# The first blocks of the last down products as half-array pairs, put between and behind the last gate groups

## The chip, the cores and the metric

The kernel runs on one core of one Trainium2 chip. The metric is the device time of one execution in microseconds; the time of a kernel is the median of several runs. Before the change it is 202.91 us, from three runs of 202.81 to 202.94. A profile is one execution recorded instruction by instruction; its span runs from the first to the last recorded instruction.

## The reference

The reference is a transformer block on an input `x` of 2048 tokens by 448 columns in bf16: a layer norm and a linear attention with 16 heads, added to `x` to give `h`, and then the part that the change touches, a gated feed-forward layer on the normed `h` with 1792 inner columns:

```
def _B_ref(x, w_gate, w_up, w_down):
    g = jnp.einsum("bsd,df->bsf", x, w_gate)
    u = jnp.einsum("bsd,df->bsf", x, w_up)
    h = _sigmoid(g) * u
    return jnp.einsum("bsf,fd->bsd", h, w_down)
...
h2 = h + _B_ref(_layernorm(h, axis=-1), B_w_gate, B_w_up, B_w_down)
```

## The kernel before

**Tiles.** The 2048 tokens are 16 tiles of 128 (tile 0 to 15), the 1792 inner columns 14 blocks of 128 (called `ff`, 0 to 13). The feed-forward part of the last four tiles, 12 to 15, is what the change touches.

**A gate group** (`gate_up`, lines 895 to 917) computes g and u of one `ff` for several tiles at once, four (512 tokens) at the end of the kernel. The contraction over 448 columns is done on half of TensorE's rows at a time: a matmul on rows 0 to 63 and one on rows 64 to 127 run beside each other, each into a bank of PSUM of its own. Line 333, in the helper `both`, issues these pairs. Operation `ga12_8` is the first part of the group of tiles 12 to 15 and `ff` 8 (four pairs), `gb12_8` the second (three pairs), with the banks exchanged between the halves. Even `ff` use banks 4 and 5, odd ones banks 0 and 1. ScalarE then takes the sigmoid of g (`sig12_8`, line 909), and VectorE multiplies it with u (`hh12_8`, line 915) and writes the product, transposed as it already is, into `hhT`. After that the two banks are free for the group of `ff` + 2.

**A down product** multiplies `hhT` with `w_down` and sums over all 14 `ff` in one bank for each tile. For tiles 0 to 11 it is done by `down` (lines 919 to 934) for two tiles at once in half-array pairs: operations `dn10_4`, `dp10_4` and so on, where the lower rows work for one tile and the upper rows for the other, and in a second pass the other way round. For tiles 12 to 15 `down1` (lines 936 to 946) does one tile at a time with matmuls on all 128 rows, issued by line 942. The 14 `ff` are split by the list `late` into blocks of 4, 4, 2, 2, 1 and 1, with names by tile and first `ff`: `dm13_8` is tile 13, `ff` 8 and 9. The banks are 2, 3, 6 and 7 for tiles 12 to 15. Tile 15 is split by columns: 320 of them as `dm15_*` in bank 7, the last 128 as `dl15_0` and `dl15_12` in bank 4. VectorE then adds the bank to `h` (`fin12`, line 949), and SyncE's queue writes the tile out (`out12`, line 952).

**Order.** The order of the operations on each engine is written out by hand in the table `ORDER` (lines 243 to 302), by name. `PROGRAM` (lines 311 to 319) creates the operations. `Graph` finds from what each operation reads and writes which others it depends on, and gives it waits on semaphores where the two are on different engines. TensorE waits for itself only where two operations write the same bank from different halves of the array (`crosses`, lines 85 to 87, from the argument `half`); an operation on the full array has an empty `half` and takes no such wait.

The order on TensorE around the change, before it:

```
dp10_8 ga12_9 dp10_11 ga12_8 gb12_9 gb12_8 dm13_0 dm12_0 ga12_11 ga12_10 gb12_11 gb12_10 dm14_0 dm15_0
dm14_4 dm13_4 ga12_13 ga12_12 gb12_13 gb12_12 dm13_8 dm12_4 dm13_10 dm15_4 dm15_8 dm12_8 dm13_12 dm12_10
dm12_12 dm12_13 dm13_13 dm14_8 dm14_10 dm14_12 dm14_13 dm15_10 dm15_12 dm15_13 dl15_0 dl15_12
```

Of the kernel before, what the change touches and what calls it, by code (L numbers as in the profile page):

```python
# [18 lines left out]
class Graph:  # L19
# [10 lines left out]
    def op(self, eng, name, fn, r=(), w=(), dma=None, nring=0, after=(), rows=128, half=None, kb=0, grp=None, many=None):  # L30
        o = _Op()
        o.engs = eng if isinstance(eng, tuple) else (eng,)
        fns = fn if isinstance(fn, tuple) else (fn,) * len(o.engs)
        k = o.engs.index(self.where[name]) if name in self.where else 0
        o.i, o.eng, o.name, o.fn, o.dma = len(self.ops), o.engs[k], name, fns[k], dma
        o.rows, o.half, o.kb, o.grp = rows, half or {}, kb, grp
        o.deps = {}
        r, w = self.flat(r), self.flat(w)
        o.need_inc, o.sem, o.val = False, None, 0

        def dep(j, raw):
            if j != o.i:
                o.deps[j] = o.deps.get(j, False) or raw
        for k in r:
            if k in self.lastw:
                dep(self.lastw[k], True)
            for j in self.adds.get(k, ()):
                dep(j, True)
        for k in w:
            if k in self.lastw:  # L50
                dep(self.lastw[k], True)
            for j in self.readers.get(k, ()):
                dep(j, False)
            if grp is None:
                for j in self.adds.pop(k, ()):
                    dep(j, True)
        for j in after:
            dep(j, False)
        if dma is not None and nring:
            lst = self.ring.setdefault(dma, [])  # L60
            if len(lst) >= nring:
                dep(lst[-nring], True)
            o.sem = (dma, len(lst) % nring)
            o.val = 16 * (len(lst) // nring + 1)
            lst.append(o.i)
        if many is not None:
            o.sem, o.val = (dma,) + many[:1], 16 * many[1]
        for k in w:
            if grp is not None:
                self.adds.setdefault(k, []).append(o.i)  # L70
                continue
            self.lastw[k] = o.i
            self.readers[k] = []
        for k in r:
            if k not in w:
                self.readers.setdefault(k, []).append(o.i)
        self.ops.append(o)
        return o.i
# [50 lines left out]
    def emit(self, nc):  # L129
# [87 lines left out]
D = 448  # L217
# [12 lines left out]
LO, HI = slice(0, 64), slice(64, P)  # L230
# [32 lines left out]
    ),  # L263
# [22 lines left out]
    ),  # L286
    "dve": (
# [14 lines left out]
    ),  # L302
    "pool": (
# [15 lines left out]
)  # L319


# [6 lines left out]
def both(e, lo, hi):  # L328
    for a in range(max(len(lo), len(hi))):
        for l, row in ((lo, 0), (hi, 64)):  # L330
            if a < len(l):
                o, w, r, st, sp = l[a]
                p = e.matmul(o, lhsT=w, rhs=r, start=st, stop=sp, tile_position=(row, 0))  # L333
    return p
# [15 lines left out]
def build(nc, A_x, A_wqkv, A_w_phi, A_wo, B_w_gate, B_w_up, B_w_down, out):  # L350
# [8 lines left out]
    NX, NO, NH, NPHI, NS, NE, NV, NSG, NHH = 5, 4, 3, 4, 4, 5, 5, 4, 2  # L359

    with ExitStack() as es:
        def sb(name, shape, d=dt.bfloat16):
            return es.enter_context(nc.sbuf_tensor(name, shape, d))
# [34 lines left out]
        wd_sb = sb("wd_sb", [P, FT, D])  # L398
# [3 lines left out]
        hhT = [sb("hhT%d" % c, [P, FT, 512]) for c in range(NHH)]  # L402
# [16 lines left out]
        def bk(i):  # L419
            return psum[:, i * 512:(i + 1) * 512]  # L420
# [4 lines left out]
        def TS(t):  # L425
            return slice((t % 4) * P, (t % 4 + 1) * P)
        g = Graph()
        op = g.op

        def B(i):  # L430
            return ("bank", i)

        def load(name, dst, src, w, kb, r=(), eng="sp", many=None):
# [9 lines left out]
           r=["ident"], w=["ident"])  # L443
# [20 lines left out]
        def opads(e):  # L464
# [4 lines left out]
           w=[("phi", s) for s in range(NPHI)])  # L469
        op("pool", "wqpad", lambda e: e.memset(W2[1][:].rearrange("p k g n -> p (k g) n")[:, :, 56:64], 0.0),  # L470
           w=[("W2", 1, kt) for kt in range(KT)])
        op("dve", "mask2", lambda e: e.tensor_reduce(mask2[:], ident[:].rearrange("p (c h) -> p h c", h=2), AX.X, ALU.add),
           r=["ident"], w=["mask2"])
# [445 lines left out]
        def down(t, b, parts):  # L919
            c = (t // 4) % NHH  # L920
            hb = hhT[c]
            for ph, a, n in parts:
                i, j = ph, 1 - ph

                def f(e, ph=ph, i=i, j=j, a=a, n=n):
                    def part(i, s):
                        return [(bk(b[i])[:, 0:D], hb[s, ff, TS(t + i)], wd_sb[s, ff, :], ph == 0 and ff == 0,
                                 ph == 1 and ff == FT - 1) for ff in range(a, a + n)]
                    return both(e, part(i, LO), part(j, HI))
                op("pe", "d%s%d_%d" % ("np"[ph], t, a), f,  # L930
                   r=[("hh", c, ff, (t + i) % 4) for ff in range(a, a + n) for i in range(2)] + [("wd", ff // 2) for ff in range(a, a + n)],
                   w=[B(b[0]), B(b[1])], rows=64, half={b[i]: 0, b[j]: 1})
            for i in range(2):
                finish(t + i, b[i])

        def down1(t, b, parts, w=0):
            hb = hhT[(t // 4) % NHH]
            for nm, b, lo, hi in (("dm", b, 0, D - w), ("dl", 4, D - w, D))[:1 + (w > 0)]:
                for a, n in parts if nm == "dm" else ((0, 12), (12, 2)):
                    def f(e, a=a, n=n, b=b, lo=lo, hi=hi):  # L940
                        for ff in range(a, a + n):
                            p = e.matmul(bk(b)[:, lo:hi], lhsT=hb[:, ff, TS(t)], rhs=wd_sb[:, ff, lo:hi], start=ff == 0, stop=ff == FT - 1)  # L942
                        return p
                    op("pe", "%s%d_%d" % (nm, t, a), f,
                       r=[("hh", (t // 4) % NHH, ff, t % 4) for ff in range(a, a + n)] + [("wd", ff // 2) for ff in range(a, a + n)], w=[B(b)])
                finish(t, b, lo, hi, "" if nm == "dm" else "b")
# [6 lines left out]

        mid = [(ph, a, n) for ph in range(2) for a, n in ((0, 4), (4, 4), (8, 3), (11, 3))]
        late = ((0, 4), (4, 4), (8, 2), (10, 2), (12, 1), (13, 1))

        for step in PROGRAM.split():
            k, _, v = step.partition(":")
            v = [int(i) for i in v.split(",") if i]
            if k == "num":  # L960
                num(*v)
            elif k == "wo":
                wout(v[0])
            elif k == "ot":
                otrans(v[0])
            elif k == "wo1":
                wout1(v[0])
            elif k == "qs":
                qsum(v[0])
            elif k == "pq":  # L970
                pq(*v)
            elif k == "kvz":
                kvmask()
            elif k == "gu":
                for ff in range(*(v[2:4] or (0, FT))):
                    gate_up(v[0], v[1], ff)
            elif k == "down":
                down(v[0], (v[1], v[1] + 1), mid)
            elif k == "down1":
                down1(v[0], v[1], late, *v[2:])  # L980

        at = {o.name: o.i for o in g.ops}
        for a, b in PACE.items():
# [5 lines left out]
def bass_sequential_preLN__linear_kernel_hedgehog__glu_gated_glu__prompt_kernel(  # L989
    nc, A_x, A_wqkv, A_w_phi, A_wo, B_x, B_w_gate, B_w_up, B_w_down, out  # L990
):
    build(nc, A_x, A_wqkv, A_w_phi, A_wo, B_w_gate, B_w_up, B_w_down, out)
# [28 lines left out]
```

## Time and profile before

| | us |
|---|---|
| median of three runs | 202.91 |
| the profiled execution | 203.01 |
| its span | 200.8 |
| TensorE busy in it | 195.0 |
| VectorE busy | 127.0 |
| ScalarE busy | 100.0 |
| GpSimd busy | 69.7 |

The profiled execution's own time is longer than its span by what lies around the instructions, about 2.2 us. PE is TensorE's matmuls and PEld its weight loads, which run beside them; DVE is VectorE, ACT ScalarE, POOL GpSimd, SP SyncE, and SPq the queue of transfers that SyncE issues. Matmuls are pipelined: one starts before the one ahead of it has ended, so the time that a matmul costs is read from the distance of starts and not from its duration. L333 is line 333 of the kernel. A timeline row gives the start, the time from the first start to the last end of the instructions merged in it, the engine, the line, the operation with its tiles, the count, and in brackets the engine's idle time ahead of it with what ended it.

### The profile page before, as it was taken

The numbers are of one execution on the slowest core, as the hardware profiler recorded it, in microseconds if no ns is written. First come the engines' busy times: TensorE is split into PE (matmuls) and PEld (weight loads), VectorE is DVE, ScalarE is ACT, GpSimd is POOL, SyncE is SP. The second block draws the span as 40 slices with busy tenths as digits, with TensorE's granted clock in tenths as the row PEclk, the third lists the DMA queues.
The fourth block names the chain that finished last, engine by engine and source line by source line (L and its number), as shares of the span: only waits on it lengthen the run. The fifth ranks groups of instructions, "written<-read, shape, count | busy, mean of one in ns | idle before, by whom it ended". The sixth has DMA issues, their size and how long they took to land.

```text
span 200.8 us, 5873 instructions
## 1 busy us (share of the span) xinstructions
PE 195.0 (97%) x2500; PEld 113.3 (56%) x2500; DVE 127.0 (63%) x309; ACT 100.0 (50%) x213; POOL 69.7 (35%) x107
## 2 busy tenths in 40 slices
PE   7899999999989999999999999999999999999994
PEld 2735555566557788886555444444555555553453
DVE  6899999978889876286558775246233522362224
ACT  3778989899795776356232543232323212221220
POOL 4599977643444456353303146100310000000000
PEclk9999999999999999999999999999999999999999
DMA  6996725469942583214102204103020000003002
GB/s 150 331 137 125 84 51 127 118 212 287 343 55 45 124 123 54 54 34 77 40 17 68 53 3 99 35 0 96 3 52 3 0 0 3 0 19 122 0 0 91
DMA packets 32866, 16.25 MB, mean 81 GB/s; under 512 B 25097, under 2 KB 31945, under 8 KB 32841
## 3 DMA queue, kind: packets, MB, share of 16 engines
q1 hardware_dynamic: 32336, 15.86, 36.5%
q8 instruction: 19, 0.31, 0.6%
q10 hardware_dynamic: 504, 0.03, 0.2%
q14 instruction: 7, 0.05, 0.1%
HBM read 8.34 MB, written 1.84 MB: 51 GB/s over the span
## 4 chain that ended last, share of the span: by engine, by line
PE 92%; DVE 3%; DMA 2%; SPq 1%; issue 1%
PE psum L333 84%; PE psum L942 5%; DMA wk_sb<-in_A_wqkv_dram 2%; PE psum L622 1%; SPq L434 1%; PE psum L531 1%; DVE c_sb L803 1%; DVE st L828 1%; PE psum L545 0%; DVE b_sb L800 0%; DVE hn_pad L850 0%; DVE xnT L538 0%; PE psum L606 0%; DVE x_sb L830 0%; DVE rsm L797 0%
## 5 line engine op out<-in xcount | busy, mean ns | idle before, releaser
L333 PE MATMUL psum<-xnT,wg_sb 64*128 64x512 bf16 (+1 forms) x490 | 95.0, 333 | 0.3 <-DVE xnT L538 0.3
L333 PE MATMUL psum<-xnT,wu_sb 64*128 64x512 bf16 (+1 forms) x490 | 94.9, 333 | 0.1
L909 ACT ACTIVATE sg_sb<-psum 128x512 bf16<-128x512 f32 (+1 forms) x70 | 35.5, 515 | 76.0 <-PE psum L333 75.6
L915 DVE TENSOR_TENSOR hhT<-sg_sb,psum 128x512 bf16<-128x512 bf16 (+1 forms) x44 | 29.2, 675 | 46.3 <-ACT sg_sb L909 45.8
L333 PEld LDWEIGHTS psum<-xnT,wg_sb 64*128 64x128 bf16 x490 | 44.5, 94 | 20.9 <-DVE hhT L915 1.1
L333 PEld LDWEIGHTS psum<-xnT,wu_sb 64*128 64x128 bf16 x490 | 44.5, 94 | 14.2 <-PE psum L333 0.9
L333 PE MATMUL psum<-wd_sb,hhT 64*128 64x448 bf16 x336 | 37.8, 349 | 0.0
L333 PEld LDWEIGHTS psum<-wd_sb,hhT 64*128 64x128 bf16 x336 | 17.9, 94 | 14.3 <-DVE x_sb L835 0.3
L333 PE MATMUL psum<-wv_sb,xnT 64*128 64x448 bf16 x112 | 22.3, 351 | 0.1
L333 PE MATMUL psum<-Wk,xnT 64*128 64x448 bf16 x112 | 22.2, 351 | 0.1
L809 POOL TENSOR_TENSOR o_pad<-c_sb,rden 128x448 bf16<-128x448 bf16 x12 | 11.2, 937 | 26.4 <-DVE rden L805 26.0
L682 POOL TENSOR_TENSOR phi<-hhT,rs 128x896 bf16<-128x896 bf16 x10 | 17.0, 1708 | 3.0 <-DVE rs L678 1.7
L672 DVE TENSOR_REDUCE ss<-hhT 128x32 f32<-128x896 bf16 x16 | 17.1, 1066 | 0.3 <-ACT hhT L669 0.2
L720 ACT ACTIVATE eq<-psum 120x1024 bf16<-120x1024 f32 x16 | 15.8, 1030 | 0.9 <-PE psum L333 0.9
L333 PE MATMUL psum<-xnT,Wq 64*120 64x512 bf16 x112 | 14.8, 384 | 0.1
L949 DVE SCALAR_TENSOR_TENSOR x_sb<-psum,x_sb 128x448 bf16<-128x448 f32 (+2 forms) x17 | 9.6, 594 | 8.1 <-PE psum L333 5.7
L914 ACT CAST xn_pad<-psum 128x256 bf16<-128x256 f32 x26 | 9.4, 375 | 6.3 <-PE psum L333 5.8
L333 PE MATMUL psum<-wo_o,oT 64*128 64x448 bf16 x49 | 11.5, 349 | 0.0
L333 PE MATMUL psum<-wo_e,oT 64*128 64x448 bf16 x49 | 11.5, 349 | 0.0
L915 POOL TENSOR_TENSOR hhT<-sg_sb,xn_pad 128x256 bf16<-128x256 bf16 x11 | 7.6, 695 | 11.1 <-ACT xn_pad L914 6.9
L942 PE MATMUL psum<-wd_sb,hhT 128*128 128x448 bf16 (+2 forms) x70 | 11.1, 316 | 0.0
L333 PEld LDWEIGHTS psum<-Wk,xnT 64*128 64x128 bf16 x112 | 7.7, 94 | 5.6 <-PE psum L333 1.0
(112 smaller groups left out, 251.3 us busy)
## 6 DMA issues: line engine op xcount, KB each, us to landing
out_dram<-x_sb SPq DMA_DIRECT2D x15, 112.0 KB, 1.8
x_sb<-in_A_x_dram SPq DMA_DIRECT2D x7, 224.0 KB, 4.9
wd_sb<-in_B_w_down_dram SPq DMA_DIRECT2D x7, 224.0 KB, 7.7
wg_sb<-in_B_w_gate_dram SPq DMA_DIRECT2D x3, 448.0 KB, 4.6
wu_sb<-in_B_w_up_dram SPq DMA_DIRECT2D x3, 448.0 KB, 4.8
wv_sb<-in_A_wqkv_dram SPq DMA_DIRECT2D x2, 224.0 KB, 5.7
wk_sb<-in_A_wqkv_dram SPq DMA_DIRECT2D x2, 196.0 KB, 3.8
wo_e<-in_A_wo_dram SPq DMA_DIRECT2D x1, 336.0 KB, 3.5
```

The lines of the kernel that those rows point to most:

```text
L333: p = e.matmul(o, lhsT=w, rhs=r, start=st, stop=sp, tile_position=(row, 0))
L434: return op(eng, name, lambda e: e.dma_start(dst, src), r=r, w=w, dma="in" if eng == "sp" else "ain", nring=(48 if eng == "sp" else 8) if ...
L531: p = e.matmul(bk(3)[:, 0:size], lhsT=zero[:, 0:P], rhs=zero[:, 0:size], start=True, stop=True)
L672: op("dve", "ss%d" % t, lambda e: e.tensor_reduce(ss[:, s, :].rearrange("p (b h) -> p b h", h=2), eks.rearrange("p b (d h) -> p b h d", h= ...
L682: return e.tensor_tensor(phi[:, sp, :, :, :].rearrange("p b a n -> p (b a) n")[:, :, 0:56].rearrange("p b (d h) -> p b d h", h=2), eks.rea ...
L720: op("act", "eq%d_%d%s" % (c, i, "pm"[sg]), lambda e, sg=sg: e.activation(eq[c][:, sg, 2 * i:2 * i + 2, :].rearrange("p g n -> p (g n)"), ...
L809: return e.tensor_tensor(o_pad[:, t % NO, off:off + D].rearrange("p (h d) -> p h d", h=H), c_sb[:, t % NS, :, 0:DH], rden[:, t % NS, :][:, ...
L909: op("act", "sig" + nm, lambda e: e.activation(sg_sb[:, k, 0:N], bk(bg)[:, 0:N], ACT.Sigmoid), r=[B(bg)], w=[("sg", k)])
L914: op("act", "uc" + nm, lambda e: e.copy(up, bk(bu)[:, 0:N]), r=[B(bu)], w=[ub])
L915: op(("pool", "dve") if nm in UCOPY else "dve", "hh" + nm, lambda e: e.tensor_tensor(hhT[(t0 // 4) % NHH][:, ff, ns], sg_sb[:, k, 0:N], up ...
L942: p = e.matmul(bk(b)[:, lo:hi], lhsT=hb[:, ff, TS(t)], rhs=wd_sb[:, ff, lo:hi], start=ff == 0, stop=ff == FT - 1)
L949: op("dve", "fin%d%s" % (t, nm), lambda e: e.scalar_tensor_tensor(out=h_sb[:, t, lo:hi], in0=bk(b)[:, lo:hi], scalar=1.0, in1=h_sb[:, t, l ...
```

## The change

Of tiles 12, 13 and 14 the first blocks of the down product (`ff` 0 to 7 of tile 12, 0 to 9 of tiles 13 and 14) are no longer full-array matmuls. A new function `downh` makes half-array pairs of two tiles: the lower 64 rows of each `ff` for one tile, the upper 64 rows for the other. The list `HALF` takes the three tiles in turn (12 with 13, 13 with 14, 14 with 12 or 13), so that each tile gets both halves of each of its `ff`. Banks stay 2, 3 and 6. The rest of these tiles and all of tile 15 stay with `down1`; the new table `left` says how many blocks it skips.

The new operations are placed on TensorE in the order below: two behind `gb12_8`, three behind `gb12_10`, two between `gb12_12` and `gb12_13`, one behind `gb12_13`. The last two gate groups change places, `dm15_0` moves behind the last gate group, and `dm13_13` moves ahead of `dm12_12`. On ScalarE and VectorE the places of `ff` 4 and 5 are exchanged, on ScalarE those of 10 and 11 too; on VectorE `fin11` moves ahead of `hh12_9`, `fin10` between `hh12_9` and `hh12_8`, and `fin13` ahead of `fin12`. SyncE's order stays.

```diff
 "act":
-        "sig12_0 sig12_2 sig12_3 sig12_4 sig12_5 sig12_7 sig12_6 sig12_9 sig12_8 sig12_10 sig12_11 sig12_12 sig12_13 "
+        "sig12_0 sig12_2 sig12_3 sig12_5 sig12_4 sig12_7 sig12_6 sig12_9 sig12_8 sig12_11 sig12_10 sig12_12 sig12_13 "
 "pe":
-        "dp10_8 ga12_9 dp10_11 ga12_8 gb12_9 gb12_8 dm13_0 dm12_0 ga12_11 ga12_10 gb12_11 gb12_10 dm14_0 dm15_0 "
-        "dm14_4 dm13_4 ga12_13 ga12_12 gb12_13 gb12_12 dm13_8 dm12_4 dm13_10 dm15_4 dm15_8 dm12_8 dm13_12 dm12_10 "
-        "dm12_12 dm12_13 dm13_13 dm14_8 dm14_10 dm14_12 dm14_13 dm15_10 dm15_12 dm15_13 dl15_0 dl15_12 "
+        "dp10_8 ga12_9 dp10_11 ga12_8 gb12_9 gb12_8 dx1213_0 dx1213_4 ga12_11 ga12_10 gb12_11 gb12_10 dx1314_0 "
+        "dx1314_4 dx1314_8 ga12_12 ga12_13 gb12_12 dx1412_0 dx1412_4 gb12_13 dx1413_8 dm15_0 dm12_8 dm13_10 dm15_4 "
+        "dm13_12 dm15_8 dm12_10 dm13_13 dm12_12 dm12_13 dm14_10 dm14_12 dm14_13 dm15_10 dm15_12 dm15_13 dl15_0 "
+        "dl15_12 "
 "dve":
-        "hh8_9 hh8_8 hh8_11 hh8_10 hh8_13 fin6 fin7 hh8_12 hh12_1 hh12_0 hh12_2 hh12_3 hh12_4 hh12_5 fin9 hh12_7 fin8 "
-        "hh12_6 fin10 fin11 hh12_9 hh12_8 hh12_10 hh12_11 hh12_12 hh12_13 fin12 fin13 fin14 fin15 fin15b "
+        "hh8_9 hh8_8 hh8_11 hh8_10 hh8_13 fin6 fin7 hh8_12 hh12_1 hh12_0 hh12_2 hh12_3 hh12_5 hh12_4 fin9 hh12_7 fin8 "
+        "hh12_6 fin11 hh12_9 fin10 hh12_8 hh12_10 hh12_11 hh12_12 hh12_13 fin13 fin12 fin14 fin15 fin15b "
 PROGRAM:
-    "down:10,6 gu:12,4 down1:12,2 down1:13,3 down1:14,6 down1:15,7,128 "
+    "down:10,6 gu:12,4 half down1:12,2 down1:13,3 down1:14,6 down1:15,7,128 "
+HALF = (
+    (12, 13, 0, 4), (12, 13, 4, 4), (13, 14, 0, 4), (13, 14, 4, 4), (13, 14, 8, 2), (14, 12, 0, 4), (14, 12, 4, 4),
+    (14, 13, 8, 2),
+)
...
+        def downh(lo, hi, a, n):
+            hb, bank = hhT[(lo // 4) % NHH], {12: 2, 13: 3, 14: 6}
+            first = {t: next(p for p in HALF if t in p[:2] and p[2] == 0) for t in (lo, hi)}
+
+            def f(e):
+                def part(t, s):
+                    return [(bk(bank[t])[:, 0:D], hb[s, ff, TS(t)], wd_sb[s, ff, :], ff == 0 and first[t] == (lo, hi, a, n), False)
+                            for ff in range(a, a + n)]
+                return both(e, part(lo, LO), part(hi, HI))
+            op("pe", "dx%d%d_%d" % (lo, hi, a), f,
+               r=[("hh", (lo // 4) % NHH, ff, t % 4) for ff in range(a, a + n) for t in (lo, hi)] + [("wd", ff // 2) for ff in range(a, a + n)],
+               w=[B(bank[lo]), B(bank[hi])], rows=64, half={bank[lo]: 0, bank[hi]: 1})
...
+        left = {12: 2, 13: 3, 14: 3, 15: 0}
...
+            elif k == "half":
+                for p in HALF:
+                    downh(*p)
             elif k == "down1":
-                down1(v[0], v[1], late, *v[2:])
+                down1(v[0], v[1], late[left[v[0]]:], *v[2:])
```

## The prediction

> **What bounds the kernel now.** The page is read first for the engine that sets the end. The lines below are its span, its busy shares, the granted clock and the chain that ended last.
>
> ```profile
> span 200.8 us, 5873 instructions
> PE 195.0 (97%) x2500; PEld 113.3 (56%) x2500; DVE 127.0 (63%) x309; ACT 100.0 (50%) x213; POOL 69.7 (35%) x107
> PEclk9999999999999999999999999999999999999999
> PE 92%; DVE 3%; DMA 2%; SPq 1%; issue 1%
> ```
>
> TensorE is busy for 195.0 of 200.8 us, holds 92% of the chain, and its clock is full in every slice. So time is won only if TensorE's own sequence gets shorter. The chain in order of time shows which part of it the change touches:
>
> ```profile
> 119.94 61.11 PE psum L333 x594
> 181.05 1.62 PE psum L942 x8
> 182.67 3.13 PE psum L333 x28
> 185.80 2.92 PE psum L942 x16
> 188.72 3.13 PE psum L333 x28
> 191.85 6.42 PE psum L942 x46
> ...
> 198.29 0.29 DVE x_sb L949
> ```
>
> From 119.94 us on the chain is TensorE alone. L333 is the helper that issues half-array pairs (64 rows each, two in flight on the two halves), L942 the full-array matmul (128 rows). Up to 181.05 only pairs run. Then full-array blocks of 8, 16 and 46 alternate with two gate stretches of 28. The tile sizes change five times: pair to full at 181, back, to full at 185.8, back, and to full at 191.85. The change works exactly here, so I read TensorE's timeline at these joins; columns are start, duration, engine, line, operation, count. First a join without a change of tile size, gate pairs to down pairs and back:
>
> ```profile
> 170.83 0.38 PE L333 MATMUL psum<-xnT,wu_sb 64*128 64x512 bf16 x1
> ...
> 171.05 2.07 PE L333 MATMUL psum<-wd_sb,hhT 64*128 64x448 bf16 x20
> 172.94 0.38 PE L333 MATMUL psum<-xnT,wg_sb 64*128 64x512 bf16 x1
> ...
> 173.16 0.38 PE L333 MATMUL psum<-xnT,wg_sb 64*128 64x512 bf16 x1
> ```
>
> Ten down pairs (20 matmuls) take 171.05 to 172.94: 1.89 us, 0.189 us a pair, and gate pairs stand 0.22 apart on both sides. This join costs nothing. Now, from the same view, the three joins to full-array blocks and the two back:
>
> ```profile
> 180.66 0.38 PE L333 MATMUL psum<-xnT,wu_sb 64*128 64x512 bf16 x1
> ...
> 180.98 1.69 PE L942 MATMUL psum<-wd_sb,hhT 128*128 128x448 bf16 x8
> 182.60 0.39 PE L333 MATMUL psum<-xnT,wg_sb 64*128 64x512 bf16 x1
> ...
> 182.83 0.38 PE L333 MATMUL psum<-xnT,wg_sb 64*128 64x512 bf16 x1
> ...
> 185.42 0.38 PE L333 MATMUL psum<-xnT,wu_sb 64*128 64x512 bf16 x1
> ...
> 185.73 2.99 PE L942 MATMUL psum<-wd_sb,hhT 128*128 128x448 bf16 x16
> 188.65 0.39 PE L333 MATMUL psum<-xnT,wg_sb 64*128 64x512 bf16 x1
> ...
> 188.88 0.38 PE L333 MATMUL psum<-xnT,wg_sb 64*128 64x512 bf16 x1
> ...
> 191.47 0.38 PE L333 MATMUL psum<-xnT,wu_sb 64*128 64x512 bf16 x1
> 191.78 6.47 PE L942 MATMUL psum<-wd_sb,hhT 128*128 128x448 bf16 x46
> ```
>
> The steady gate pitch is (185.42 - 182.83) / 12 = 0.216 us. But the full-array blocks start 0.32, 0.31 and 0.31 us after the last gate pair, and the first gate pair after a block takes 0.23. The steady pitch of full matmuls comes from a row inside the last block:
>
> ```profile
> 195.63 1.30 PE L942 MATMUL psum<-wd_sb,hhT 128*128 128x448 bf16 x6
> ```
>
> and the duration of one from the view that groups instructions by form (busy, mean ns):
>
> ```profile
> L942 PE MATMUL psum<-wd_sb,hhT 128*128 128x448 bf16 x42 | 8.8, 353 | 0.0
> ```
>
> Six matmuls take 1.30 us and the last of them lasts 0.353: (1.30 - 0.353) / 5 = 0.189 us, the same as a pair. Between 191.78 and 195.63 lie 16 matmuls of 448 columns and 6 of 320 (tile 15's): (3.85 - 16 x 0.189) / 6 = 0.138 us for one of 320.
>
> **The change, part by part.** Counts are from the diff. The 8 new operations hold 4+4+4+4+2+4+4+2 = 28 pairs, and `left` drops 8 blocks of tile 12, 10 of 13 and 10 of 14: 28 full matmuls of 448 columns go. 28 pairs come for 28 full matmuls, each 0.189 us: the work term is **0**. How exact that is: the pair pitch is read over ten (0.01 us of 1.89) and the full one over five, so 0.002 us each way per pair, +-0.06 in all.
>
> What goes are joins. The new order has only pairs up to the last gate group: 8 pairs before group 11/10, 10 pairs before 12/13, 8 pairs between the gb of group 12 and that of 13, 2 behind. One join to full-array matmuls stays, before dm15_0. What the four lost joins cost:
> - First gap, 180.66 to 182.83: 2.17 us. Without joins two gate pitches and 8 matmuls, 2 x 0.216 + 8 x 0.189 = 1.944. Excess **0.226**.
> - Second gap, 185.42 to 188.88: 3.46 us. Two gate pitches, 12 of 448 and 4 of 320 (dm15_0), 0.432 + 2.268 + 0.552 = 3.252. Excess **0.208**.
>
> The two make 0.434 us, and twice the first, which is free of the 320 pitch, makes 0.452. Readings of 0.01 per gap give 0.41 to 0.46; I take **-0.44**, 0.11 a join. The fifth join (0.31 - 0.216 = 0.09) is in both kernels.
>
> The Trainium skill, TensorEngine Tiling, Key Properties, says that changing the tiling mode drains TensorE, while changing only the tile does not. The trace agrees that only a change of size pays; but a drain to the end of the last matmul would be an estimated 0.16 a join and 0.66 in all (rival B), where these rows show 0.11. The sum above goes by the rows.
>
> What would the moved work uncover? Gate groups use banks 4/5 (even) and 0/1 (odd), and a ga waits until VectorE's hh of the group two before has read its banks. Three covers shrink or shift:
>
> ```profile
> 178.93 0.63 DVE L949 SCALAR_TENSOR_TENSOR x_sb<-psum,x_sb 128x448 bf16<-128x448 f32 x1 [0.68 <-PE psum L333]
> 181.07 0.69 DVE L915 TENSOR_TENSOR hhT<-sg_sb,psum 128x512 bf16<-128x512 bf16 x1 [0.98 <-ACT sg_sb L909]
> 181.72 0.69 DVE L915 TENSOR_TENSOR hhT<-sg_sb,psum 128x512 bf16<-128x512 bf16 x1
> 185.84 0.60 ACT L909 ACTIVATE sg_sb<-psum 128x512 bf16<-128x512 f32 x1 [4.16 <-PE psum L333]
> 186.47 0.69 DVE L915 TENSOR_TENSOR hhT<-sg_sb,psum 128x512 bf16<-128x512 bf16 x1 [4.06 <-ACT sg_sb L909]
> ...
> 56.82 0.75 DVE L538 COPY xnT<-psum 128x512 bf16<-128x512 bf16 x2
> 57.71 0.27 PE L333 MATMUL psum<-xnT,wg_sb 64*128 64x256 bf16 x1 [0.26 <-DVE xnT L538]
> ```
>
> The last two rows give the way from VectorE to TensorE: 57.57 to 57.71, 0.14 us.
> - **fin10 now stands between hh12_9 and hh12_8.** hh12_9 still starts at 181.07, fin10 at 181.72, hh12_8 some 0.6 later at 182.3, done 183.0, seen 183.15. ga12_11 wants 180.88 + 8 x 0.189 = 182.39, ga12_10 four gate pitches later, 183.25. Hidden, with 0.1 to spare. fin11 is put ahead and starts at 178.93.
> - **Before group 12/13 the cover falls from 16 matmuls to 10 pairs.** With t0 the start of the last pair of gb12_10, ga12_12 wants t0 + 0.216 + 1.89 = t0 + 2.11. sig12_11 now goes first, on an operation that ends three gate pitches earlier, so sig12_10 still starts 0.42 after t0 (185.84 for 185.42), hh12_10 at +1.05, done +1.74, seen +1.88. Hidden, with 0.23 to spare. ga12_13, 0.86 later, waits for hh12_11, one 0.61 behind: more room.
> - **sig12_5 before sig12_4** leaves hh12_5 at its time and puts hh12_4 behind it. The later hh of two is done some 2.4 after the last gate pair's start (1.74 + 0.65) and seen at 2.5; ga12_6 wants its banks after 0.216 + ten down pairs + a ga, 0.216 + 1.89 + 0.86 = 2.97. Hidden.
>
> Waits that are added: a dx whose bank was last written by the other array half waits on TensorE itself (dx1314_0 for dx1213_4, dx1412_0 and dx1413_8 for dx1314). Behind each stands all of TensorE, but what is awaited lies a gate group of 2.4 us or more back, or eight pairs. dx1314_0 also waits for fin10, which ends at 182.35 and is needed near 185.4; dm15_0 for fin11. hh12_13 is seen 1.88 after the start of the last gate pair; dm13_13, the first to need it, comes after 2 pairs, a join, 7 matmuls of 448 and 10 of 320: 0.216 + 0.378 + 0.09 + 1.32 + 1.38 = 3.39. Hidden.
>
> On the queues: SP's out10 waits for fin10 and holds out7, 8, 9, 6 and 11 behind it; all move from 179.58 to some 182.4.
>
> ```profile
> 182.70 0.92 SPq L952 DMA_DIRECT2D out_dram<-x_sb  x2
> 196.89 0.33 SPq L952 DMA_DIRECT2D out_dram<-x_sb  x1
> 195.64 0.62 DVE L949 SCALAR_TENSOR_TENSOR x_sb<-psum,x_sb 128x448 bf16<-128x448 f32 x1 [1.84 <-PE psum L942]
> 196.97 0.62 DVE L949 SCALAR_TENSOR_TENSOR x_sb<-psum,x_sb 128x448 bf16<-128x448 f32 x1 [0.17 <-PE psum L942]
> ```
>
> Today the last two of these six are out by 183.62; 2.8 later is still ten before out13 at 196.89. Nobody waits: 0. At the end dm12_13 comes three matmuls (0.57) nearer to the end, so fin12 starts at 196.2 on today's scale instead of 195.64, with fin13 ahead of it; fin14, released at 196.97, has 0.17 of idle ahead of it that takes this up, and the end hangs on fin15b behind dl15_12 as now. Cost 0; without that idle, a few hundredths, still absorbed by the idle before fin15b.
>
> **Sum.** The profiled execution took 203.01 us (span 200.8 and 2.2 around it), 0.10 above the median of the three runs, 202.91. I expect the change to shorten it to 203.01 - 0.44 = 202.57, span 200.36, and the median to **202.47**.
>
> **The rivals.**
> - **A: the pair costs more than a full matmul.** The two of a pair start 0.01 to 0.02 us apart. If 0.01 were paid for each of the 28 pairs, 0.28 is given back: 202.75. Against it: ten pairs in 1.89 us show no such addition. Chance 0.08. The Trainium skill, TensorE: Matmul & The Clock Gate, Measured speedup vs the span model, gives about 4 ns per further tile of a packed group; by that the estimate is 28 x 4 ns = 0.11, and 202.58; the rows above show less.
> - **B: a join drains TensorE completely.** Then a lost join is worth a matmul's full duration less its pitch, 0.38 - 0.216 or 0.353 - 0.189, 0.164 each: 4 x 0.164 = 0.66, 202.25. Against it: the block at 180.98 begins before the 0.38 us from 180.68 or 180.66 are over (181.04), and the measured excess is 0.11 per join. Chance 0.04. The Trainium skill's rule on the tiling mode, named above, would read so if the drain lasts to the matmul's end.
> - **C: the change doesn't do what it says.** If the pauses come from the waits of the blocks (a bank, an hh) and not from the size, they move with the blocks: 202.9. For it: the view of waits (us in total, times, longest) puts one pause of the weight loads down to VectorE:
>
> ```profile
> PEld psum L942 <- issue: 1.3, 3, 0.4
> ...
> PEld psum L333 <- DVE hhT L915: 0.4, 1, 0.4
> ```
>
> Against it: down pairs with the same kinds of waits joined at 171.05 without pause, and the pauses are alike (0.4 each) although their releasers aren't. Chance 0.08.
> - **D, on the other side: ga12_12 waits for its banks.** The place is the second gap, where the cover falls from 3.0 to 1.89 us. The price is one for one beyond the 0.23 to spare; it eats the gain at 0.44 + 0.23 = 0.67 us of delay of hh12_10, and passes slower by 0.2% at 1.08. If hh12_10 came behind a further hh and a fin on VectorE (0.69 + 0.62 = 1.31), the stall is 1.08: 202.47 + 1.08 = 203.55. Against it: fin10 and hh12_8 are done some 3 us before. Chance 0.06.
>
> **How the numbers follow.** The forecast has 0.74, between 202.38 and 202.56 (the pitches' +-0.06 and the runs' own spread). A measurement of this kernel can tell 0.2%, 0.41 us, from no change: below 202.50 is faster. The forecast lies 0.03 below that line, so about three quarters of its chance are faster, 0.55, and 0.19 the same. With B faster has 0.59; with A and C the same has 0.35; slower has D's 0.06. The range is 202.25 to 202.75: the forecast, A, B.
>
> **What would show it.** The chain's end should hold one L942 block of 42 (14 of 448, 14 of 320, 14 of 128) instead of 8, 16 and 46; L333's down pairs 392 matmuls for 336; PE 2528. The first dx after a gate pair should start 0.22 after it and not 0.31, and the next gate pair 0.189 after the last dx pair. Any idle of TensorE at ga12_10 or ga12_12 with VectorE as releaser would be D; eight pairs over 1.51 us would be A. The prediction is wrong if the L942 block starts less than 0.35 us earlier against the gate work, or if the span falls by less than that.

## The result

| | before | changed |
|---|---|---|
| median of 8 runs, us | 202.86 | 202.02 |
| lowest and highest, us | 202.39, 203.38 | 201.40, 202.40 |
| span of the profiled execution, us | 200.8 | 199.5 |

The ratio of the times is 0.996, with a 95% interval of 0.9943 to 0.9978: 0.81 us faster, between 0.45 and 1.16. The forecast was 0.44 faster, 202.47, with a range down to 202.25; the kernel is faster, as forecast, but by almost twice as much.

The chain of waits of the changed kernel, its last rows (start, duration, what):

```profile
119.25 0.05 issue
119.30 72.45 PE psum L338 x706
191.75 5.45 PE psum L960 x42
197.20 0.02 issue
197.23 0.29 DVE x_sb L967
```

The lines have moved (L338 is the pair helper, L960 the full-array matmul, L967 the fin), but the reading is the same. (In the kernel before, the table ORDER reaches to line 311 and PROGRAM begins at 314, not where the section on the kernel has them.) One block of 42 full-array matmuls has taken the place of 8, 16 and 46; everything ahead of it is pairs. TensorE's timeline at the former joins:

```profile
180.02 0.38 PE L338 MATMUL psum<-xnT,wu_sb 64*128 64x512 bf16 x1
...
180.24 1.69 PE L338 MATMUL psum<-wd_sb,hhT 64*128 64x448 bf16 x16
181.75 0.38 PE L338 MATMUL psum<-xnT,wg_sb 64*128 64x512 bf16 x1
...
181.97 0.38 PE L338 MATMUL psum<-xnT,wg_sb 64*128 64x512 bf16 x1
...
184.56 0.38 PE L338 MATMUL psum<-xnT,wu_sb 64*128 64x512 bf16 x1
...
184.77 2.07 PE L338 MATMUL psum<-wd_sb,hhT 64*128 64x448 bf16 x20
186.66 0.38 PE L338 MATMUL psum<-xnT,wg_sb 64*128 64x512 bf16 x1
...
188.82 0.38 PE L338 MATMUL psum<-xnT,wu_sb 64*128 64x512 bf16 x1
...
189.04 1.69 PE L338 MATMUL psum<-wd_sb,hhT 64*128 64x448 bf16 x16
190.55 0.38 PE L338 MATMUL psum<-xnT,wu_sb 64*128 64x512 bf16 x1
```

Each dx block starts 0.21 or 0.22 us after the gate pair ahead of it, and eight pairs take 1.51 us, ten 1.89. The pauses at these joins are gone, and a pair costs what a full matmul did.

Where did the rest come from? The two profiles lie 1.3 us apart, more than the medians, in part by luck: the changed kernel's is of its fastest execution, 201.40. I split each profile at two points: the start of the chain's last long stretch of pairs (119.94 before, 119.30 after), and the end of fin15b (198.29 + 0.29 = 198.58 before, 197.23 + 0.29 = 197.52 after).

| us | before | changed | difference |
|---|---|---|---|
| up to the last stretch of pairs (**start**) | 119.94 | 119.30 | -0.64 |
| from there to the end of fin15b (**body**) | 78.64 | 78.22 | -0.42 |
| from there to the end of the span (**end**) | 2.22 | 1.98 | -0.24 |

The body gives 0.42, against the 0.44 (0.41 to 0.46) that the joins were priced at. The start holds nothing whose order the change touches. The end had been priced at nothing. It shows on SyncE's queue, whose last five issues are out13, out12, out14, out15 and out15b in both kernels. Before (the first, at 196.89, stands in the prediction):

```profile
197.27 0.42 SPq L952 DMA_DIRECT2D out_dram<-x_sb  x1
197.75 0.43 SPq L952 DMA_DIRECT2D out_dram<-x_sb  x1
198.22 0.45 SPq L952 DMA_DIRECT2D out_dram<-x_sb  x1
198.72 0.46 SPq L952 DMA_DIRECT2D out_dram<-x_sb  x1
```

and in the changed kernel:

```profile
195.49 0.33 SPq L970 DMA_DIRECT2D out_dram<-x_sb  x1
195.95 0.34 SPq L970 DMA_DIRECT2D out_dram<-x_sb  x1
196.55 0.33 SPq L970 DMA_DIRECT2D out_dram<-x_sb  x1
196.97 0.40 SPq L970 DMA_DIRECT2D out_dram<-x_sb  x1
197.54 0.33 SPq L970 DMA_DIRECT2D out_dram<-x_sb  x1
```

Before, out13 was first on the queue and waited for fin13, which VectorE did second, at 196.18 to 196.79. The finished out12 stood behind it.

```profile
196.18 0.61 DVE L949 SCALAR_TENSOR_TENSOR x_sb<-psum,x_sb 128x448 bf16<-128x448 f32 x1
```

From 196.89 on the five issues follow each other with gaps of 0.04 to 0.06, so the queue itself is the bound: out15b goes out at 198.72, 0.14 after fin15b. In the changed kernel fin13 comes first, the issues are spread over the fins, and out15b goes out at 197.54, 0.02 after fin15b. So 0.12 of the 0.24 is the later issue. The other 0.12 lies in the issue itself, which took 0.46 us before and takes 0.33 now. That part shows again in the time from the start of the issue to the landing, 1.6 us before and 1.5 after; the view of transfers has it so:

```profile
out_dram<-x_sb SPq DMA_DIRECT2D x1, 32.0 KB, 1.6
```

```profile
out_dram<-x_sb SPq DMA_DIRECT2D x1, 32.0 KB, 1.5
```

### The profile page after: what moved, and what is told of

Same layout as the page of the kernel before. It is cut to its first block, busy times and chain, and to the rows that moved or that the text cites. A ratio compares the mean times of both kernels' runs of the same rounds, so it can differ in the third digit from the quotient of the medians.

```text
span 199.5 us, 5929 instructions
## 1 busy us (share of the span) xinstructions
PE 194.7 (98%) x2528; PEld 114.3 (57%) x2528; DVE 126.8 (64%) x309; ACT 100.0 (50%) x213; POOL 69.5 (35%) x107
## 4 chain that ended last, share of the span: by engine, by line
PE 92%; DVE 3%; DMA 2%; SPq 1%; issue 1%
PE psum L338 87%; PE psum L960 3%; DMA wk_sb<-in_A_wqkv_dram 2%; PE psum L627 1%; SPq L439 1%; PE psum L536 1%; DVE c_sb L808 1%; DVE st L833 1%; PE psum L550 0%; DVE b_sb L805 0%; DVE hn_pad L855 0%; DVE xnT L543 0%; PE psum L611 0%; DVE x_sb L835 0%; DVE rsm L802 0%
## 5 line engine op out<-in xcount | busy, mean ns | idle before, releaser
L338 PE MATMUL psum<-xnT,wg_sb 64*128 64x512 bf16 (+1 forms) x490 | 95.1, 333 | 0.3 <-DVE xnT L543 0.3
L338 PE MATMUL psum<-xnT,wu_sb 64*128 64x512 bf16 (+1 forms) x490 | 95.0, 333 | 0.1
L338 PEld LDWEIGHTS psum<-xnT,wg_sb 64*128 64x128 bf16 x490 | 44.7, 94 | 20.3 <-DVE hhT L920 0.8
L338 PEld LDWEIGHTS psum<-xnT,wu_sb 64*128 64x128 bf16 x490 | 44.6, 94 | 14.0 <-PE psum L338 0.9
L338 PE MATMUL psum<-wd_sb,hhT 64*128 64x448 bf16 x392 | 43.8, 349 | 0.0
L338 PEld LDWEIGHTS psum<-wd_sb,hhT 64*128 64x128 bf16 x392 | 20.9, 94 | 16.8 <-DVE x_sb L840 0.3
L338 PE MATMUL psum<-wv_sb,xnT 64*128 64x448 bf16 x112 | 22.2, 351 | 0.1
L338 PE MATMUL psum<-Wk,xnT 64*128 64x448 bf16 x112 | 22.1, 350 | 0.1
L338 PE MATMUL psum<-xnT,Wq 64*120 64x512 bf16 x112 | 14.8, 384 | 0.1
L967 DVE SCALAR_TENSOR_TENSOR x_sb<-psum,x_sb 128x448 bf16<-128x448 f32 (+2 forms) x17 | 9.7, 594 | 7.5 <-PE psum L338 5.1
L338 PE MATMUL psum<-wo_o,oT 64*128 64x448 bf16 x49 | 11.5, 349 | 0.0
L338 PE MATMUL psum<-wo_e,oT 64*128 64x448 bf16 x49 | 11.5, 349 | 0.0
L338 PEld LDWEIGHTS psum<-Wk,xnT 64*128 64x128 bf16 x112 | 7.7, 94 | 5.5 <-PE psum L338 1.0
L805 DVE TENSOR_TENSOR b_sb<-psum,qq 128x464 bf16<-128x464 f32 x16 | 10.1, 634 | 0.7 <-PE psum L338 0.4
```

The source lines that it names most:

```text
L805: op("dve", "b%d" % t, lambda e: e.tensor_tensor(h3(b_sb), OMv[:, :, :, 0:EV], h2(qq)[:, :, :, None].to_broadcast([P, NB, 8, EV]), ALU.mul ...
L967: op("dve", "fin%d%s" % (t, nm), lambda e: e.scalar_tensor_tensor(out=h_sb[:, t, lo:hi], in0=bk(b)[:, lo:hi], scalar=1.0, in1=h_sb[:, t, l ...
```

## The experiments

The theory after the result: **J** and **Q**, the joins in the body (0.42 us) and the queue at the end (0.24), 0.66 together; the rest is the spread of the start. The expectations of e1 to e4 know only J. The rivals: **L**, the longer program (28 more matmuls) shifts the start for good, and **grown B**, a lost join is worth 0.2 us in executions that are timed without a profile being kept.

All profiles split as above, with the measured ratio to the kernel before in the same rounds. "Change by profile" is body plus end against 78.64 + 2.22.

| kernel | start | body | end | change by profile, us | measured ratio (95%) |
|---|---|---|---|---|---|
| before, again (e2) | 119.65 | 78.64 | 2.21 | -0.01 | 1.0000 (0.9983 to 1.0018) |
| before, third (e10) | 119.50 | 78.64 | 2.26 | 0.04 | 0.9997 (0.9980 to 1.0013) |
| changed, again (e1) | 119.44 | 78.21 | 1.95 | -0.70 | 0.9959 (0.9943 to 0.9975) |
| changed, third (e9) | 119.25 | 78.22 | 1.93 | -0.71 | 0.9963 (0.9949 to 0.9976) |
| one trip put back (e3) | 120.27 | 78.43 | 2.00 | -0.43 | 0.9986 (0.9971 to 1.0000) |
| three trips put in (e4) | 119.83 | 78.86 | 2.01 | 0.01 | 0.9989 (0.9977 to 1.0001) |
| before, out12 first (e6) | 119.24 | 78.64 | 2.02 | -0.20 | 0.9977 (0.9965 to 0.9989) |
| the same again (e11) | 119.50 | 78.64 | 1.96 | -0.26 | 0.9980 (0.9966 to 0.9995) |
| before, fin13 first (e12) | 120.29 | 78.64 | 1.97 | -0.25 | 0.9984 (0.9970 to 0.9999) |
| changed, old end (e7) | 119.62 | 78.22 | 2.56 | -0.08 | 0.9996 (0.9982 to 1.0010) |
| changed, ld_k2 first (e5) | 120.39 | 78.22 | 1.99 | -0.65 | 1.0014 (1.0000 to 1.0027) |
| before, ld_k2 first (e8) | 120.49 | 78.64 | 2.27 | 0.05 | 1.0044 (1.0025 to 1.0064) |

A thousandth is 0.2 us. The span is given to a tenth, so the end is good to 0.05. With the unrounded spans of the same traces, body plus end is 80.84 to 80.86 in the four profiles of kernels with the old joins and the old end, 80.18 to 80.19 in the four of the changed one and of e5, and 80.60 to 80.61 in e6, e11 and e12.

**The same kernels again (e1, e2, then e9, e10).** No edit. Expected for the first two:

> The changed kernel once more. Theory J: the change is worth its four lost joins, 0.43 us, and the further 0.4 of the first comparison is the spread of the start, where the second load of wk_sb landed 0.65 us sooner in the one profile than in the other. Then the median is 0.43 us (0.3 to 0.6) under the kernel before in these rounds, and the stretch from TensorE's last whole run of pairs to the end is 0.42 shorter in any profile, whatever its start. Rival L: the longer program (28 more matmuls) shifts the start for good; then it is 0.85 under, and the profile shows the second load of wk_sb landing 3.8 us after its issue again. Rival B of the prediction, grown: a lost join is worth 0.2 us when no profile runs; then also 0.85 under, with any start.

> The kernel before against itself: what the comparison gives for no change. All theories: 0, within 0.2 us. Theory J: the landing of the second load of wk_sb in the profile moves by some tenths of a us from the 4.47 of the first profile. Rival L: it lands 4.4 to 4.5 us after its issue again.

The changed kernel is 0.83 us faster (0.51 to 1.15), the kernel before equal to itself. The body is the same to 0.01 us in every profile of a kernel, and the end to 0.05. The start isn't: 119.94 and 119.65 before, 119.30 and 119.44 changed. This left L standing, so both ran a third time:

> The changed kernel a third time, for the part of its gain that is not yet explained (0.84 and 0.83 measured, 0.66 from the profiles: 0.42 joins and 0.24 queue). If the rest is the spread of the start between loads of a program, the difference lies on either side of 0.66, within 0.25, and the profile's two parts repeat: 78.2 us from the start of the last stretch of pairs to the end of fin15b, 2.0 from there to the end of the span. If the changed program starts sooner for good, 0.84 again with that stretch starting before 119.5.

> The kernel before once more beside it: 0 within 0.25 us, 78.6 us and 2.2 in the two parts, and a start of the last stretch of pairs between 119.2 and 120.3, as the seven kernels with the same loads had it.

Now 0.75 faster (0.49 to 1.03). The profiled start was again sooner in the changed kernel, 119.25 against 119.50, so the profiles of these runs don't refute L. The spans of all executions do, as told under the start (e5, e8).

**Joins by dose (e3, e4).** Both keep the changed kernel's program, 5929 instructions, and only move full-array blocks of tile 15 between the pairs on TensorE.

```diff
e3  -gb12_13 dx1413_8 dm15_0 dm12_8
    +gb12_13 dx1413_8 dm12_8
    -dx1314_8 ga12_12
    +dx1314_8 dm15_0 ga12_12
e4  -gb12_8 dx1213_0         -gb12_10 dx1314_0         -dx1412_4 gb12_13
    +gb12_8 dm15_0 dx1213_0  +gb12_10 dm15_4 dx1314_0  +dx1412_4 dm15_8 gb12_13
```

In e4 the three blocks also go from their places behind the last pairs, which this cut does not show; its table is one line shorter, so L337, L959 and L966 are the changed kernel's L338, L960 and L967.

> The changed kernel with dm15_0, four full-array matmuls of 320 columns, moved back from behind the last gate group into the second gap, behind dx1314_8. The work is the same; two joins more. Theory J: 0.21 us slower than the changed kernel, 0.22 faster than before; in the profile 0.2 more between the gate pairs around that gap. Rival L (start): the same 0.2 for the joins, but 0.64 faster than before. Grown B: 0.43 faster than before.

> The changed kernel with dm15_0 ahead of the first dx, dm15_4 ahead of the dx behind gb12_10 and dm15_8 in the third gap behind dx1412_4: three trips to the full array and back, six joins more than the changed kernel and two more than the kernel before, with the program length of the changed one. Theory J: 0.65 us slower than the changed kernel and 0.2 slower than before. Rival L: 0.2 faster than before. Grown B: 1.3 slower than the changed kernel and 0.4 slower than before.

The chain of waits of e4:

```profile
119.83 61.12 PE psum L337 x594
180.95 0.65 PE psum L959 x4
181.59 4.64 PE psum L337 x44
186.24 0.65 PE psum L959 x4
186.89 5.89 PE psum L337 x58
192.77 0.38 PE psum L959 x2
193.15 1.13 PE psum L337 x10
194.28 4.09 PE psum L959 x32
198.38 0.02 issue
198.40 0.29 DVE x_sb L966
```

The body grows by 0.21 us for one trip and 0.64 for three: 0.21 a trip, 0.107 a join, whether 4 or 2 matmuls stand between the joins. So J is shown in the body. Grown B speaks of the measured times: against the changed kernel in the same rounds e4 is 0.61 us slower, where J asked for 0.65 and grown B for 1.3, each ratio being good to some 0.3 us. So e4 refutes it. e3 is 0.55 slower, which does not tell J's 0.21 from grown B's 0.43. Against before, e3 and e4 are 0.28 and 0.22 faster. This lies within 0.25 of what the profiles say (-0.43 and 0.01), though not within what theory J alone expected for e4, 0.2 slower: e3 and e4 keep the changed kernel's end, 2.0, and that is what J alone had left out. They also speak against L. Their program is as long as the changed kernel's, and their starts are 120.27 and 119.83, among the later ones, while the shorter program of e6 started at 119.24.

**The queue alone (e6, e11, e12).** The kernel before, first with two entries exchanged on SyncE's queue, then with the changed kernel's order on TensorE and VectorE at the end; no pairs in either.

```diff
e6, e11  -oT14 oT15 hT13 ... out11 out13 out12 out14
         +oT14 oT15 hT13 ... out11 out12 out13 out14
e12      -dm12_10 dm12_12 dm12_13 dm13_13 dm14_8     -fin12 fin13 fin14
         +dm12_10 dm13_13 dm12_12 dm12_13 dm14_8     +fin13 fin12 fin14
```

> The kernel before with one thing changed: out12 ahead of out13 on SyncE's queue, as VectorE finishes fin12 first there. Theory Q (the last five issues stood back to back on the queue, and out15b came late through them): the first of the last five issues starts 0.6 earlier, out15b is issued 0.02 after fin15b instead of 0.14, from the end of fin15b to the end of the span it takes 2.0 us instead of 2.2, and the kernel is 0.2 us faster. If only joins and start count: 0, and 2.2 stays.

> The kernel before with out12 ahead of out13, once more: the first comparison gave 0.47 where its profile showed 0.20. If the queue is worth what the profile shows, 0.20 with 0.25 either way; if it costs more in executions that no profile records, 0.47 again.

> The kernel before with the end of the changed one as the only edit: dm13_13 ahead of dm12_12 on TensorE and fin13 ahead of fin12 on VectorE, no half-array pairs and the joins as before. Theory Q: 78.64 us from the last stretch of pairs to the end of fin15b, as before, and 2.0 behind it instead of 2.24; 0.24 faster than before, with 0.25 either way. If the queue counts for nothing: 0.

The body stays at 78.64 in all three and the end falls from 2.2 to 2.0: the queue is worth 0.20 to 0.26 by the profiles (0.24 in each of the three by the unrounded spans), without any pair. The queue rows of e6 show how:

```profile
195.66 0.33 SPq L952 DMA_DIRECT2D out_dram<-x_sb  x1
196.13 0.34 SPq L952 DMA_DIRECT2D out_dram<-x_sb  x1
196.92 0.33 SPq L952 DMA_DIRECT2D out_dram<-x_sb  x1
197.33 0.40 SPq L952 DMA_DIRECT2D out_dram<-x_sb  x1
197.92 0.33 SPq L952 DMA_DIRECT2D out_dram<-x_sb  x1
```

fin15b ended at 197.59 + 0.29 = 197.88, and out15b was issued 0.04 later. The measured gains are 0.47, 0.40 and 0.32, larger than the profiles' each time. The intervals of e11 and e12 reach down to 0.10 and 0.02; that of e6 ends at 0.22, just above its profile's 0.20.

**The changed kernel with the old end (e7).**

```diff
-dm12_10 dm13_13 dm12_12 dm12_13 dm14_10     -fin13 fin12 fin14
+dm12_10 dm12_12 dm12_13 dm13_13 dm14_10     +fin12 fin13 fin14
```

> The changed kernel with the old end: dm13_13 behind dm12_13 again and fin12 ahead of fin13; the queue still has out13 first. Theory Q: from the end of fin15b to the end of the span 2.2 us again, 0.2 slower than the changed kernel, 0.42 under the kernel before. If only joins and start count: as the changed kernel, 2.0 and 0.65 to 0.84 under.

It came out worse than expected, equal to the kernel before. The joins' 0.42 is there (body 78.22), but the end takes 2.56. The queue rows:

```profile
196.53 0.33 SPq L970 DMA_DIRECT2D out_dram<-x_sb  x1
196.91 0.42 SPq L970 DMA_DIRECT2D out_dram<-x_sb  x1
197.38 0.44 SPq L970 DMA_DIRECT2D out_dram<-x_sb  x1
197.87 0.45 SPq L970 DMA_DIRECT2D out_dram<-x_sb  x1
198.37 0.45 SPq L970 DMA_DIRECT2D out_dram<-x_sb  x1
```

fin15b ended at 197.84, and out15b was issued 0.53 later. Without dm14_8 the fins of 12 and 13 fall nearer to the end, the five issues start 1.31 us before fin15b's end instead of 1.69, and five in a row take as long as ever. That is the queue at a third dose: lag 0.02, 0.14 and 0.53, end 1.98, 2.22 and 2.56. With the old order at the end the half-array pairs gain 0.08 us, which the measurement can't tell from nothing.

**The start (e5, e8).** One edit, on the changed kernel and on the kernel before:

```diff
-x1 x0 ld_k0 x2 ld_k2 x4
+x1 x0 ld_k0 ld_k2 x2 x4
```

> The changed kernel with the load ld_k2 (second half of wk_sb) issued ahead of x2 on SyncE's queue. Theory S (the rest of the difference between runs is the start): TensorE no longer waits for that load, its long run of pairs starts at 17.6 to 17.8 us or earlier in the profile, and the kernel is 0.1 to 0.4 us faster than the changed one, so 0.8 to 1.1 under the kernel before, with less spread. If the start is not the cause: as the changed kernel, 0.65 to 0.84 under.

> The kernel before with ld_k2 ahead of x2 as the only change. Theory S: 0.1 to 0.4 us faster than before, and between this and the changed kernel with the same edit lie 0.65 us, the joins' 0.42 and the queue's 0.23. Rival L (the longer program shifts the start): 0.85 between the two.

My expectation that this shortens the start was wrong: both are slower, and the chain now waits for the load that was put back.

```profile
2.60 4.17 DMA x_sb<-in_A_x_dram
```

With the same start edit on both sides, the kernels lie 1.0044 - 1.0014 = 0.0030 apart, 0.61 us; body and end give 0.42 + 0.28 = 0.70, L asked for 0.85. With some half a microsecond of interval either way this does not tell the two apart.

What answers L is the span of every execution, which is on record. Body and end repeat in every profile of a kernel, so the span less the two gives each execution's start, if they repeat in the others too. By this the changed kernel's starts average 119.72 in its 20 executions, and those of the kernel before 119.70 in the 98 that it ran beside the experiments, each mean good to 0.15. The longer program does not start sooner, and the sooner starts of its three profiles were luck. What is left of L is small and lies outside the span: an execution's time less its span averages 1.91 to 1.94 us in the seven sets of runs of the longer program and 1.95 to 2.0 in the ten of the shorter. These 0.05 us no row explains.

No version tried beats the changed kernel.

## Why the prediction was right or wrong

**The lost joins: right.** Predicted 0.44 with 0.41 to 0.46, measured 0.42 in the body, 0.107 a join against the 0.11 read from the starts. The Trainium skill, TensorEngine Tiling (Array Packing), Key Properties, says that a change of the tiling mode drains TensorE. The trace agrees that the change costs, at 0.107 us a join. Rival B took the pause to the end of the matmul, 0.164 a join: one trip would then have added 0.33 us to the body, and e3 added 0.21.

**The work term of 0: right.** Eight pairs take 1.51 us and ten 1.89, 0.189 a pair. Rival A, with 0.01 a pair, would show as 1.59 for eight. The Trainium skill, TensorE: Matmul & The Clock Gate, Measured speedup vs the span model, gives about 4 ns for each further tile of a packed group. By that figure the estimate for eight pairs is 1.54, and the trace shows 1.51.

**The covers: right.** ga12_12 starts at 186.66, 2.10 after the start of the last pair of gb12_10 (184.56), as worked out (2.11). In the view of waits of the changed kernel from 165 us on, one row is left for TensorE and its weight loads, the one join:

```profile
PEld psum L960 <- issue: 0.4, 1, 0.4
```

Rival D did not come. Rival C is out too: the pauses went with the joins, and came back with them in e3 and e4.

**The end: the step that failed.** The prediction said that "the end hangs on fin15b behind dl15_12 as now. Cost 0". Its "Nobody waits: 0" was said of six earlier transfers. It followed VectorE's fins to the end and never laid out the five issues behind them, although the start of the first, 196.89, was quoted. Five issues, 0.38 to 0.50 from start to start, take from 196.89 to 199.18, and fin15b ends at 198.58: the queue was late, and the exchange of fin12 and fin13 with the blocks ahead of them, put at no cost in the prediction, is what freed it (e12). Its size is 0.24 us by the profile. That the exchange was part of the change was luck: without it nearly all of the joins' gain is lost there, 0.42 less 0.34 by e7's end (2.56 against 2.22).

With this term the forecast is 202.86 - 0.44 - 0.24 = 202.18 from the median of the same rounds; measured 202.02, with 201.70 to 202.41 by the interval. The changed kernel's three comparisons gave 0.81, 0.83 and 0.75 against 0.66 to 0.71 by the profiles, each interval holding the latter.

**What stays open.** The remaining 0.1 of these comparisons is within the spread of the start, which runs from 119.24 to 120.29 in the twelve profiles of kernels with the same loads. Over all executions whose span is on record the changed kernel's mean, 201.83 of 20, lies 0.68 under that of the kernel before, 202.51 of 98: 0.63 of it is span, where body and end ask for 0.66. The queue's kernels gained 0.1 to 0.3 more than their profiles show, and that stays open. Their shortest spans, 199.7, 199.8 and 199.8, lie 0.2 to 0.3 under the 200.0 of the kernel before, as the profiles say, but their means lie 0.43 under it. Either their starts came sooner by chance, or the queue costs more in the slower executions. The four profiles with the kernel before's end speak against the latter: they give 2.2 for starts from 119.50 to 120.49.

## What to carry to other kernels

Price a change of order to the very end of the span: after the last compute instruction come the issues on the queue, and if they stand back to back, a transfer that waits at the head of an in-order queue for a result that comes second delays all behind it. Half-array and full-array matmuls of the same work cost the same here, and what costs is going from one to the other, 0.11 us each way; so group the work by tile size. When a small gain is measured, split every profile into start, body and end: the body repeated to 0.01 us here while the whole execution spread by half a microsecond and more.

## What the runs showed of the hardware that had not been expected

At the end of these kernels a transfer issue on SyncE's queue took 0.33 or 0.34 us when the queue had been idle for 0.13 or more ahead of it, 0.40 after 0.09, and 0.42 to 0.46 when it followed another within 0.06 us (rows of the kernel before, the changed one and e7), so a backlog lengthens itself. The small out15b, 32 KB, shows both, 0.33 and 0.46. And the start of one and the same kernel moved by 0.44 us between profiles (119.94, 119.65, 119.50 in the kernel before), through the landing of the second load of wk_sb among others: 4.47 us after its issue in the first profile of before, 3.82 in that of the changed kernel, and 4.81 in e3:

```profile
2.60 4.81 DMA wk_sb<-in_A_wqkv_dram
```
